# Sinkhorn block attention into a SwiGLU layer: batch 0's values over both row halves, queries drained inside Sinkhorn, one unit's x channel-major, wider weight loads

## The chip, the core and the metric

The kernel runs on one core of one Trainium2 chip. The core has TensorE (matrix products, called PE in the profile, its weight loads PEld), VectorE (DVE), ScalarE (ACT), GpSimd (POOL) and SyncE (SP, which here only issues DMAs), and 16 DMA engines that all queues share. The metric is device time in microseconds of one execution of the whole program, as the median of several runs.

## The reference

q, k and v are 4 batches x 8 heads x 768 positions x 64 channels. Each sequence is cut into 8 blocks of 96 positions. `sort_net` (8x8 for each head) goes through five Sinkhorn steps (exponential, row sum to one, column sum to one) and becomes a mixing matrix P, which mixes the blocks of k and v. Attention then runs inside each block, and the result, with the heads side by side (512 features), is the input of a gated feed-forward layer of width 1536.

```python
for _ in range(5):
    P = P - np.max(P, axis=-1, keepdims=True)
    P = np.exp(P)
    P = P / (np.sum(P, axis=-1, keepdims=True) + 1e-09)
    P = P / (np.sum(P, axis=-2, keepdims=True) + 1e-09)
k_sorted = np.einsum('bhij,bhjcd->bhicd', P, k_b)
v_sorted = np.einsum('bhij,bhjcd->bhicd', P, v_b)
scores = scale * np.matmul(q_b, k_sb.transpose(0, 1, 2, 4, 3))
attn = softmax(scores)
x = np.matmul(attn, v_sb)          # then (B*S, H*D)
out = (silu(x @ w_gate) * (x @ w_val)) @ w_out
```

Inputs and outputs are float32; the kernel works in bfloat16 with float32 sums.

## The kernel before, in words

**Layout.** Rows are (head, block) pairs: 64 of them, so a batch fills one half of the 128 partitions (`lowr`, `highr`). A mixing step is a matmul of natural rows of k or v with `rmix`, a 64x64 matrix that holds P of each head on its diagonal blocks. q is brought into the same channel-major layout by a selection matrix `sel`. For v the positions must come out on the partitions, so v is first copied to `vch` with channels outside and positions inside (`copy_v`, lines 117 to 124), and then mixed channel by channel (`v_chunk`, from line 267). k and q of batch 0 are split over both row halves already (`k0_chunk`, `q0_chunk`). Mixed v lies in `vt` with a column of ones behind each block, so that the product with the exponentials gives the softmax sums as well.

**A unit** is four blocks of two heads; a batch has eight. `scores` and `exps` (ScalarE) give the exponentials in `e_all`; `av` (line 326) multiplies with `vt`, takes a reciprocal of eight sums, and scales into `st`; x comes out with positions on the partitions and is transposed by TensorE (`x_to`, line 347) into `xt` and drained from PSUM. Later batches transpose by DMA.

**Stages.** Half a batch (384 positions) is one feed-forward stage, `ffn(0)` to `ffn(7)`: twelve gates (`gate`), twelve values (`value`) and three output products (`outp`). `merge` puts the attention of later halves between these steps at written places (numbers in units of estimated us of feed-forward work). PSUM has two double banks (`a`, `b`), three single ones (`gen`) and one (`x`).

**The head.** Until `ffn(0)` the order on TensorE, VectorE, ScalarE and GpSimd is written out by hand; later TensorE's and GpSimd's still are. GpSimd issues all loads that cast to bfloat16, in this order: v of batch 0 in two position halves (lines 108, both onto the lower 64 rows), q (first half), k in two halves, then three of its copies of v, then the gate and value weights in twelve loads of 256 columns, with the second half of q, v, k and q of batch 1, and one load of the output weights among and behind them. At most eight GpSimd loads are under way: the ninth waits for the first. ScalarE runs Sinkhorn's five exponentials with four copies of v between and behind them (lines 195 to 220); VectorE runs the sums, reciprocals and products. TensorE keeps itself busy with idle products (`dots`, `fill`), then turns P into `rmix` (`weights`, `mix_rows`), brings up q, v and k of batch 0 in chunks that VectorE and ScalarE drain, and computes four units. `early` starts the first gates and values on three of the four 128-feature slices of x while the fourth is under way; the fourth slice is the fourth unit (`av(0, 3)`).

Two lines that the rest comes back to:

```python
nc.vector.reciprocal(r_sb, o[0:C, :, :, D:D + 1])
merge(ffn(1), vs(v_chunk, 16, (3.2, 3.9, 4.7, 5.5)) + kqs(1, (6.2, 8.2, 10.3)) + ...)
```

Of the kernel before, what the change touches and what calls it, by code (L numbers as in the profile page):

```python
# [9 lines left out]
FP32 = mybir.dt.float32  # L10
# [7 lines left out]
def kernel(  # L18
# [15 lines left out]
    C = S // NB  # L34
    BH = B * H
# [38 lines left out]
    wo_sb = wpool.tile([128, NFC, DM], BF16)  # L74
# [3 lines left out]
    e_all = const.tile([C, 8, 4 * C + 32], BF16)  # L78
# [54 lines left out]
    HC = C // 2  # L133
    QC = C // 4
# [8 lines left out]

    load_v(0, 0, HC)
    load_v(0, HC, C)
# [4 lines left out]
    copy_v(nc.gpsimd, 0, lowr, 0)  # L150
    copy_v(nc.gpsimd, 0, lowr, 3)
    copy_v(nc.gpsimd, 0, lowr, 5, 8, 40, D)
    load_gv(0, 256)
    load_q0(1)
    for m in range(256, 1024, 256):
        load_gv(m, m + 256)
    load_v(1, 0, C)
    for m in range(1024, DF, 256):
        load_gv(m, m + 256)
    load_k(1, 0, C)  # L160
    load_q(1, 0, C)
    nc.gpsimd.dma_start(out=wo_sb, in_=wo_dram)

    rmix = {b: const.tile([128, 2, H, NB], BF16, name=f"rmix{b}") for b in (0, 1, "p")}
    for t in rmix.values():
        nc.vector.memset(t, 0.0)

    vts = {}

    def vt_tile(pair):  # L170
        if pair not in vts:
            t = vtp.tile([C, 2, H * NB, D + 4], BF16, name=f"vt{pair}", tag="vt")
            nc.vector.memset(t[:, :, :, D:D + 1].rearrange("p u n e -> p (u n) e"), 1.0)
            vts[pair] = t
        return vts[pair]

    for pair in range(B // 2):
        vt_tile(pair)

# [12 lines left out]

    p_ps = bank_tile("p_ps")[0:BH, 0:NB * NB].rearrange("p (i j) -> p i j", j=NB)
    for it in range(N_ITER):
        nc.scalar.activation(p_ps, p_sb if it == 0 else p_ps, AF.Exp)
        if it == 1:
            with nc.allow_low_precision("0/1 mask"):
                nc.vector.tensor_reduce(mask, id4, axis=AX.XY, op=ALU.add)
            nc.scalar.copy(sel, ident.rearrange("p (r g two) -> p two g r", g=H2, two=2))
        if it == 2:  # L200
            copy_v(nc.scalar, 0, lowr, 2, 8)
        if it == 3:
            copy_v(nc.scalar, 0, lowr, 3, 8)
        rowred = rowreds[it]
        nc.vector.reduce_sum(rowred[:, :, 0], p_ps, axis=AX.X)
        nc.vector.reciprocal(rowred, rowred)
        nc.vector.tensor_mul(p_ps, p_ps, rowred.to_broadcast([BH, NB, NB]))
        nc.vector.reduce_sum(colred[:, 0, :], p_ps.transpose([0, 2, 1]), axis=AX.X)
        nc.vector.reciprocal(colred, colred)
        if it < N_ITER - 1:  # L210
            nc.vector.tensor_mul(p_ps, p_ps, colred.to_broadcast([BH, NB, NB]))
    for lo in (0, NB // 2):
        part = slice(lo, lo + NB // 2)
        nc.vector.tensor_tensor(
            p_bf[:, part], p_ps[:, part].unsqueeze(2).to_broadcast([BH, NB // 2, H, NB]),
            colred.unsqueeze(1).to_broadcast([BH, NB // 2, H, NB]), op=ALU.mult)
    copy_v(nc.scalar, 0, lowr, 4, 8)
    copy_v(nc.scalar, 0, lowr, 5, 8, 0, 40)

# [6 lines left out]
    kqts = {}  # L226
# [22 lines left out]
    def q0_chunk(t, at, n, eng, tag):  # L249
        dst = kqt_tile(0)[:, GI * C:2 * GI * C].rearrange("p (g t r c) -> p t g r c", g=H2, t=2, c=QC)[:, t]  # L250
# [5 lines left out]
        drain(eng, dst[:, :, :, at:at + n], tp.rearrange("p l g r -> p g r l"))  # L256
# [56 lines left out]
    def exps(b, u, wide, pss):  # L313
        n = ecount[0] % 8
        ecount[0] += 2
        if wide is None:
            for two in range(2):
                nc.scalar.activation(e_all[:, n + two, 0:4 * C], pss[two][0:C, 0:4 * C], AF.Exp, scale=scale)
# [336 lines left out]
```

## Time and profile before

| | |
|---|---|
| Median of 3 runs | 248.6 us (248.59 to 248.83) |
| Profiled execution, its own time | 249.62 us |
| Span of the profiled execution (first to last instruction) | 247.7 us |
| TensorE busy | 239.4 us (97%) |
| VectorE busy | 157.1 us (63%) |
| ScalarE busy | 109.5 us (44%) |
| GpSimd busy | 51.9 us (21%) |
| Loads by GpSimd's queue | 14.16 MB written, 39.3% of 16 engines' span |
| Mean granted TensorE clock | 1.0 of full speed |

The span is shorter than the execution's own time, since something lies before the first and behind the last instruction. A busy engine is not an engine at its peak: TensorE's busy time includes the idle products of the head. In the views, L403 is line 403; `out<-in` are the tiles that an instruction writes and reads; a number in brackets is idle time of that engine just before the instruction, with what ended it. "Issue to landing" of a DMA is the time until its data is there.

### The profile page before, as it was taken

What the parts mean: (1) busy time and instruction counts of PE and PEld (TensorE: products, weight loads), DVE (VectorE), ACT (ScalarE), POOL (GpSimd) and SP (SyncE); (2) the same over time, 40 slices, a digit from 0 to 9 for tenths busy, and PEclk for the clock granted to TensorE, in tenths of its full rate; (3) what the DMA queues carried; (4) which work ended last, traced back from release to release, by engine and by line L of the source; (5) the groups of instructions that cost most, each with busy time, mean ns of one, the idle gap of its engine ahead of it and who ended that gap; (6) DMA issues with size and microseconds to landing.
All of it is one profiled execution on the core that took longest, in us unless ns stands there. A gap on an engine that the chain in (4) does not pass through costs nothing.

```text
span 247.7 us, 6185 instructions
## 1 busy us (share of the span) xinstructions
PE 239.4 (97%) x2633; PEld 140.7 (57%) x2633; DVE 157.1 (63%) x332; ACT 109.5 (44%) x186; POOL 51.9 (21%) x45
## 2 busy tenths in 40 slices
PE   8799998999999999999999999999999999999995
PEld 6375665666555556655555655565555555555543
DVE  6686789787556775857657646755764585446700
ACT  3877652453544444444642552354245334232311
POOL 5993459960049300000000000000000000000000
PEclk9999999999999999999999999999999999999999
DMA  5999999999999287010122121112111121100122
GB/s 98 214 120 181 218 191 219 194 227 215 215 164 179 41 201 173 4 42 3 45 56 52 55 62 34 44 42 78 32 42 45 39 57 54 42 21 25 42 81 88
DMA packets 39578, 24.38 MB, mean 98 GB/s; under 512 B 27712, under 2 KB 35648, under 8 KB 39104
## 3 DMA queue, kind: packets, MB, share of 16 engines
q0 software_dynamic: 21376, 14.16, 39.3%
q1 hardware_dynamic: 18176, 9.84, 13.9%
q8 instruction: 20, 0.33, 0.5%
q14 instruction: 6, 0.05, 0.1%
HBM read 28.32 MB, written 7.86 MB: 146 GB/s over the span
## 4 chain that ended last, share of the span: by engine, by line
PE 83%; DVE 9%; ACT 2%; issue 2%; DMA 2%; DVEq 0%; POOLq 0%
PE v_ps L403 23%; PE o_ps L420 23%; PE g_ps L385 22%; PE tkq L244 3%; PE av_ps L334 2%; PE qk L307 2%; DVE st L340 2%; DMA v<-in_v_dram 2%; DVE gs_sb L395 2%; DVE h L408 2%; DVE vt L222 1%; PE o_ps L436 1%; PE idle_ps L446 1%; PE tv L275 1%; ACT th_sb L393 1%
## 5 line engine op out<-in xcount | busy, mean ns | idle before, releaser
L395 DVE SCALAR_TENSOR_TENSOR gs_sb<-th_sb,g_ps 128x384 bf16<-128x384 bf16 x96 | 52.8, 550 | 51.5 <-ACT th_sb L393 48.7
L403 PE MATMUL v_ps<-xt,wv_sb 128*128 128x384 bf16 x380 | 77.3, 326 | 1.1 <-DVE st L340 0.7
L385 PE MATMUL g_ps<-xt,wg_sb 128*128 128x384 bf16 x376 | 76.7, 326 | 0.1
L393 ACT ACTIVATE th_sb<-g_ps 128x384 bf16<-128x384 f32 x96 | 47.1, 490 | 57.0 <-PE g_ps L385 54.5
L420 PE MATMUL o_ps<-wo_sb,h 128*128 128x512 bf16 x276 | 64.0, 379 | 0.0
L408 DVE SCALAR_TENSOR_TENSOR h<-v_ps,gs_sb 128x384 bf16<-128x384 f32 x96 | 53.3, 555 | 6.9
L403 PEld LDWEIGHTS <-wv_sb 128*128 128x128 bf16 x380 | 35.1, 97 | 24.9 <-issue 1.9
L385 PEld LDWEIGHTS <-wg_sb 128*128 128x128 bf16 x376 | 34.7, 97 | 23.5 <-issue 0.4
L420 PEld LDWEIGHTS <-h 128*128 128x128 bf16 x276 | 26.3, 98 | 28.9
L425 ACT COPY o_sb<-o_ps 128x512 f32<-128x512 f32 x23 | 13.5, 585 | 50.9 <-PE o_ps L420 50.9
L124 POOL COPY vch<-v 64x1536 bf16<-64x1536 bf16 (+2 forms) x11 | 28.6, 2635 | 21.1 <-DMA v<-in_v_dram 21.0
L320 ACT ACTIVATE e_all<-qk 96x768 bf16<-96x768 f32 x30 | 22.6, 802 | 7.6 <-PE qk L307 7.6
L340 DVE TENSOR_TENSOR st<-av_ps,r_sb 96x512 bf16<-96x512 f32 x32 | 21.7, 679 | 0.2
L334 PEld LDWEIGHTS <-e_all 96*128 96x128 bf16 x256 | 12.0, 97 | 4.9 <-ACT e_all L320 0.9
L334 PE MATMUL av_ps<-vt,e_all 96*128 96x65 bf16 x256 | 13.2, 193 | 0.0
L222 DVE CAST vt<-tv 96x1024 bf16<-96x1024 f32 (+1 forms) x9 | 9.8, 1096 | 2.6 <-PE tv L285 1.6
L338 DVE RECIPROCAL r_sb<-av_ps 96x8 f32<-96x8 f32 x32 | 6.4, 199 | 8.0 <-PE av_ps L334 7.9
L224 ACT CAST vt<-tv 96x1024 bf16<-96x1024 f32 (+1 forms) x9 | 8.1, 913 | 3.0 <-PE tv L285 1.8
L446 PE MATMUL idle_ps<-warm_sb 128*128 128x512 bf16 x25 | 7.7, 416 | 0.0
L222 DVE COPY oh_sb<-o_ps 128x256 f32<-128x256 f32 x1 | 0.4, 423 | 9.3 <-PE o_ps L436 9.3
L122 ACT COPY vch<-v 64x768 bf16<-64x768 bf16 (+1 forms) x4 | 5.4, 1375 | 0.7 <-DMA v<-in_v_dram 0.7
L370 POOL DMA_DIRECT2D q_scr<-in_q_dram x2 | 5.7, 3228 | 0.0
(80 smaller groups left out, 135.3 us busy)
## 6 DMA issues: line engine op xcount, KB each, us to landing
out_dram<-o_sb SPq DMA_DIRECT2D x23, 256.0 KB, 2.0
v<-in_v_dram POOLq DMA_DIRECT2D x3, 768.0 KB, 19.9
wg_sb<-in_moe_w_gate_dram POOLq DMA_DIRECT2D x6, 256.0 KB, 11.1
wv_sb<-in_moe_w_val_dram POOLq DMA_DIRECT2D x6, 256.0 KB, 11.9
wo_sb<-in_moe_w_out_dram POOLq DMA_DIRECT2D x1, 1536.0 KB, 23.8
kp<-in_k_dram POOLq DMA_DIRECT2D x2, 768.0 KB, 15.1
q_scr<-in_q_dram POOLq DMA_DIRECT2D x2, 768.0 KB, 29.9
v<-in_v_dram POOLq DMA_DIRECT2D x2, 384.0 KB, 6.4
```

The source lines that it names most:

```text
L124: eng.tensor_copy(dst, src.transpose([0, 2, 1]))
L222: nc.vector.tensor_copy(dst, src)
L320: nc.scalar.activation(e_all[:, n:n + 2, 0:4 * C], wide[0:C, :, 0:4 * C], AF.Exp, scale=scale)
L334: nc.tensor.matmul(o[:, two, i4, 0:D + 1], lhsT=e[:, i4 * C:i4 * C + 128], rhs=vt[:, 2 * g + two, half * 4 + i4, 0:D + 1], start=True, sto ...
L340: nc.vector.tensor_tensor(st.rearrange("p i two d -> p two i d"), o[0:C, :, :, 0:D], r_sb.to_broadcast([C, 2, 4, D]), op=ALU.mult)
L385: nc.tensor.matmul(g_ps, lhsT=wg_sb[:, kc, ts(m, 128)], rhs=xt[:, kc, :], start=(kc == 0), stop=(kc == NKC - 1))
L393: nc.scalar.activation(th_sb, g_ps, AF.Tanh, scale=0.5)
L395: nc.vector.scalar_tensor_tensor(gs_sb, th_sb, 1.0, g_ps, op0=ALU.add, op1=ALU.mult)
L403: nc.tensor.matmul(v_ps, lhsT=wv_sb[:, kc, ts(m, 128)], rhs=xt[:, kc, :], start=(kc == 0), stop=(kc == NKC - 1))
L408: nc.vector.scalar_tensor_tensor(h_tiles[n][:, m, :], v_ps, 0.5, gs_tiles.pop(m), op0=ALU.mult, op1=ALU.mult)
L420: nc.tensor.matmul(o_ps, lhsT=h_w[:, m, ts(t3, 128)], rhs=wo_sb[:, m, :], start=(m == 0), stop=(m == NFC - 1))
L425: nc.scalar.copy(o_sb, o_ps)
```

## The change

- **Batch 0's values.** The first 48 positions of each block go to the lower 64 rows, the other 48 to the upper, as k's did. The copy has 48 positions instead of 96 on twice the rows: ten of them in one ScalarE copy in Sinkhorn's fourth step, 38 in two GpSimd copies. Mixing takes two 64x64 products for each channel, and mixed v has its positions on partitions 0 to 47 and 64 to 111; k of batch 0 and the exponentials are laid out to match, with zeros between (112 rows instead of 96). GpSimd writes the zeros and the ones with nine memsets ahead of its copies, and one of 2048 elements behind the weights.
- **q.** Its first two chunks (48 products) stand on TensorE before the last row-sum product of Sinkhorn, and ScalarE drains both.
- **Fourth unit.** `avt` multiplies the other way round: the result has channels on the partitions and is x itself. The softmax sums come from a product with ones, spread over the channels; VectorE takes the reciprocal of all 128x384 of them and multiplies. There is no transpose and no drain. The second value of `ffn(0)` moves into `early`.
- **Loads.** Gate and value weights come in six loads of 512 columns, all ahead of v, k and q of batch 1, which are loaded in two parts each; the output weights in three.
- **Places.** In `ffn(1)` k and q of batch 1 come ahead of v; the first part of the last two batches' v moves from `ffn(3)` to the end of `ffn(2)`; some other places move.

```diff
-    load_v(0, 0, HC)
-    load_v(0, HC, C)
+    v0 = vnp.tile([128, HC, D], BF16, name="v0", tag="vn")
+    for a, rows in enumerate(halves):
+        nc.gpsimd.dma_start(out=v0[rows], in_=v_nat[0, :, a * HC:(a + 1) * HC, :])
     make_identity(nc, ident)
     load_q0(0)
     for a, rows in enumerate(halves):
         nc.gpsimd.dma_start(out=k0[rows], in_=k_nat[0, :, a * HC:(a + 1) * HC, :])
-    copy_v(nc.gpsimd, 0, lowr, 0)
-    copy_v(nc.gpsimd, 0, lowr, 3)
-    copy_v(nc.gpsimd, 0, lowr, 5, 8, 40, D)
-    load_gv(0, 256)
+    nc.gpsimd.memset(vch0[:, :, HC:], 0.0)
+    nc.gpsimd.memset(kqt0[:, 0:NK].rearrange("p (n c) -> p n c", c=64)[:, :, HC:], 0.0)
...
+    copy_v0(nc.gpsimd, 10, 29)
+    copy_v0(nc.gpsimd, 29, HC)
+    load_gv(0, 512)
     load_q0(1)
-    for m in range(256, 1024, 256):
-        load_gv(m, m + 256)
-    load_v(1, 0, C)
-    for m in range(1024, DF, 256):
-        load_gv(m, m + 256)
-    load_k(1, 0, C)
-    load_q(1, 0, C)
-    nc.gpsimd.dma_start(out=wo_sb, in_=wo_dram)
+    load_gv(512, 1024)
+    load_gv(1024, DF)
+    nc.gpsimd.memset(vch[lowr, D * 64:D * C], 0.0)
+    load_v(1, 0, HC)
+    load_v(1, HC, C)
+    for lo, hi in ((0, 64), (64, C)):
+        load_k(1, lo, hi)
+        load_q(1, lo, hi)
+    for n in range(3):
+        nc.gpsimd.dma_start(out=wo_sb[n], in_=wo_dram[:, n * 4:(n + 1) * 4, :])
...
+    def v0_chunk(at, n, eng, tag):
+        tp = chunk_tile("tv0", n // 8, tag).rearrange("p (l n) -> p l n", n=H * NB)
+        for ld in range(n):
+            for a, rows in enumerate(halves):
+                nc.tensor.matmul(tp[rows, ld, :], lhsT=vch0[rows, at + ld, :],
+                                 rhs=rmix[0][rows, a].rearrange("p h i -> p (h i)"),
+                                 start=True, stop=True)
+        drain(eng, vts[0][0:KC, 0, :, at:at + n], tp[0:KC].transpose([0, 2, 1]))
...
+    def avt(u, tag):
+        half, g = divmod(u, H2)
+        vt = vts[0][0:KC, 0].rearrange("p (h i) e -> p h i e", h=H)
+        ps = pair_tile("avt_ps", tag)
+        for two in range(2):
+            nc.tensor.matmul(ps[two * D:(two + 1) * D, 512:512 + TW], lhsT=ones_sb[0:KC],
+                             rhs=es[(0, u)][two][:, 0:TW], start=True, stop=True)
+        for i4 in range(4):
+            for two in range(2):
+                nc.tensor.matmul(ps[two * D:(two + 1) * D, i4 * C:(i4 + 1) * C],
+                                 lhsT=vt[:, 2 * g + two, half * 4 + i4, 0:D],
+                                 rhs=es[(0, u)][two][:, i4 * C:(i4 + 1) * C], start=True, stop=True)
+        total = opool.tile([128, DM], FP32, name="total", tag="o_sb")[:, 0:TW]
+        x = xts[(0, half)][:, g, :]
+        nc.vector.reciprocal(total, ps[:, 512:512 + TW])
+        nc.vector.tensor_tensor(x, ps[:, 0:TW], total, op=ALU.mult)
...
+        if it == 3:
+            copy_v0(nc.scalar, 0, 10)
...
+        if it == N_ITER - 1:
+            early_q = [q0_chunk(0, 0, 16, "s", "b"), q0_chunk(0, 16, 8, "s", "a")]
+            for f in early_q:
+                f()
...
-    q0_chunk(0, 0, 16, "s", "b")
-    v_chunk(0, 0, 8, "v", "gen")
-    v_chunk(0, 8, 8, "s", "gen")
-    v_chunk(0, 16, 16, "v", "a")
-    v_chunk(0, 32, 8, "v", "gen")
-    v_chunk(0, 40, 16, "s", "b")
-    v_chunk(0, 56, 8, "s", "gen")
+    v0_chunk(0, 8, "v", "gen")
+    v0_chunk(8, 8, "s", "gen")
+    v0_chunk(16, 16, "v", "a")
+    v0_chunk(32, 16, "s", "b")
+    v0_chunk(48, 8, "s", "gen")
+    v0_chunk(56, 8, "v", "gen")
     k0_chunk(0, 16, "v", "a")
     k0_chunk(16, 16, "s", "b")
-    k0_chunk(32, 8, "v", "gen")
-    k0_chunk(40, 8, "s", "gen")
-    q0_chunk(0, 16, 8, "v", "a")
+    k0_chunk(32, 4, "v", "gen")
+    k0_chunk(36, 4, "s", "gen")
+    k0_chunk(40, 8, "s", "a")
...
-    av(0, 3, "b")
+    avt(3, "a")
...
-    x3 = xt_tile("x", 1)
-    x_to(x3[:, 0], 0, 3)
-    drain("v", xts[(0, 0)][:, 3:4, :], x3.rearrange("p g a b -> p g (a b)"))
     early(0, (2,))
     early(1, (2,))
-    early(2, (0,))
-    early(0, (3,))
-    early(1, (3,))
-    early(2, (1, 2, 3))
+    early(2, (0, 1))
+    for n in range(2):
+        early(n, (3,))
+    early(2, (2, 3))
+    early(3, (0, 1, 2, 3))
...
-    merge(ffn(1), vs(v_chunk, 16, (3.2, 3.9, 4.7, 5.5)) + kqs(1, (6.2, 8.2, 10.3))
-          + units(1, range(4), (11.3, 16.4), (3.1, 2.5)))
+    merge(ffn(1), kqs(1, (5.9, 7.2, 11.1)) + vs(v_chunk, 16, (8.5, 9.1, 9.8, 10.4))
+          + units(1, range(4), (12.3, 17.0), (3.1, 2.4)))
...
-    merge(ffn(2), units(1, range(4, 8), (0.0, 5.5)) + kqs("p", (13.0, 16.2, 19.4))
+    merge(ffn(2), units(1, range(4, 8), (0.0, 5.5)) + kqs("p", (13.0, 14.7, 20.7)) + v_pairs([(0, 22.5)])
           + [(13.0, lambda: q_dma(2)), (16.4, lambda: q_dma(3))])
-    merge(ffn(3), v_pairs([2.6 * n for n in range(4)]) + units(2, range(4), (9.8, 14.0)))
+    merge(ffn(3), v_pairs([(1, 0.0), (2, 5.1), (3, 6.9)]) + units(2, range(4), (9.8, 14.0)))
```

## The prediction

> **What bounds the kernel now.** I read the page first, then the chain of waits over the first 30 us, the timeline of ScalarE, GpSimd and TensorE there, the landings of the first loads, and the gaps between TensorE instructions after that. The first lines are the page's (span, busy time of each engine) and the chain's (start, duration, what):
>
> ```profile
> span 247.7 us, 6185 instructions
> PE 239.4 (97%) x2633; PEld 140.7 (57%) x2633; DVE 157.1 (63%) x332; ACT 109.5 (44%) x186; POOL 51.9 (21%) x45
> ...
> 6.54 1.51 ACT vch L122
> ...
> 11.51 0.29 PE w_ps L463 x4
> ...
> 13.27 0.69 DVE vt L222
> ...
> 23.00 0.34 PE x_ps L351 x4
> ```
>
> TensorE is the bound: 239.4 of 247.7 us, at a granted clock of 1.00 in every stretch asked for. From 25.4 us on (gates and values back to back) I summed the gaps between matmul starts that exceed the column time by over 0.1 us: 4.2 us. That is all that moved loads and retimed steps can recover. The rest of the change lies in the head before 25.4 us, where the chain runs through v's load, ScalarE's copies, Sinkhorn, the v, k and q drains, four units and the fourth unit's x. Next, timeline rows (start, duration, what; idle time before it and its cause), with the landings of v's first two loads among them:
>
> ```profile
> 6.57 6.34 POOL L124 COPY vch<-v 64x1536 bf16<-64x1536 bf16 x3 [1.97 <-DMA v<-in_v_dram]
> ...
> 7.94 0.20 ACT L195 ACTIVATE p_ps<-p_ps 32x64 f32<-32x64 f32 x1
> ...
> 9.63 0.19 ACT L195 ACTIVATE p_ps<-p_ps 32x64 f32<-32x64 f32 x1
> 9.75 2.43 ACT L122 COPY vch<-v 64x768 bf16<-64x768 bf16 x2
> ...
> DMA to landing us min/median/max: 5.2/6.4/7.5
> ...
> 10.46 1.04 PE L446 MATMUL idle_ps<-warm_sb 128*128 128x512 bf16 x4
> ...
> 12.83 0.84 PE L275 MATMUL tv<-rmix,vch 64*128 64x64 bf16 x23
> ...
> 41.99 0.28 PEld L403 LDWEIGHTS <-wv_sb 128*128 128x128 bf16 x3 [0.84 <-DMA wv_sb<-in_moe_w_val_dram]
> ```
>
> See three things. v's two loads (issued at 1.28 and 1.92) land after 5.2 and 7.5 us, at 6.5 and 9.4: today the copies start on the first half. The v matmuls start at 12.83, as the Sinkhorn weights are ready. And a weight load stands 0.84 us for the last value columns, issued at 26.9 and landed 15.1 us later.
>
> **The change part by part.** The sum is a difference, made in the profiled execution (span 247.7, its own time 249.62, so 1.9 us lie around it) and put onto the median of 248.6, 1.0 below that execution.
>
> *v over both halves.* GpSimd's copy fits 0.20 us + 1.70 ns an element (2.81 at 1536, 0.69 at 288, the same at 64 and 128 rows), so two of 1216 cost 4.5 us in place of 6.34; ScalarE's (1.49 at 768, 1.00 at 480) makes 1.27 at 640, in place of 5.4 in four. But every copy now spans both halves, so it waits for 9.42, not 6.5. GpSimd ends at 13.95 (12.91 before). ScalarE's copy stands in front of the fifth exp: 9.42 + 1.27 puts that exp at 10.7 instead of 9.63, and all behind it (p_bf at 12.9, not 11.78). GpSimd's nine new memsets (2,600 elements; 0.25 us at 128 against 0.10 at one gives 1.2 ns each, the copy's 1.7 is the other end) take 3.4 to 4.9 us from 4.6: hidden by the wait, 0.1 late at worst. The two ones-memsets leave VectorE, where they stood before Sinkhorn's first exp: nothing.
>
> *q drained inside Sinkhorn.* TensorE now has 48 q matmuls ahead of the last row-sum matmul and its fill. q lands 7.8 us after its issue at 3.00, so 10.8; 48 matmuls took 0.95, and from the row-sum matmul (10.34) to the first weights matmul (11.51) are 1.17: weights start at 13.0, end at 13.65, the two mask products (0.47) end at 14.15. The v matmuls start at 14.2: **+1.35 us**. Three bounds (q on TensorE, the exp on ScalarE, GpSimd's 13.95) lie within 0.3, so none helps alone. The two q drains (1.01 on ScalarE and 0.69 on VectorE before, among v's and k's) run on an idle ScalarE.
>
> *From v to the first scores.* Before, 12.83 to 18.59: 5.76. VectorE drains 4.3 us in place of 5.0, ScalarE 4.0 in place of 4.7. But order and buffers pass it on. v doubles to 128 matmuls; those with alternating row halves took 18 ns each (L285), those on one half 29. From the start S: second VectorE drain (1024 columns) S+1.35 to 2.57; k's first 32 matmuls want its bank, to S+3.27; k's second 32, whose drain is ScalarE's, to S+3.92; then 1.01, 0.35 and 0.58 to S+5.94, scores at S+6.1 = 20.3 (18.59 before): **+1.7**. Ends: 5.0 if the drains pack, 7.5 if 128 matmuls cost 31 ns each.
>
> *Fourth unit.* The four units' exps are a ScalarE chain that does not change: its last ends at 24.2 (22.50). Before, av, reciprocal 0.20, product 0.69, transposes 0.34 and drain 0.36 gave x at 24.74. Now two 384-column sums (0.16 to 0.33 us), 8 matmuls of 96 columns, a reciprocal of 128x384 and a product (0.555, the row of that shape). The reciprocal decides, and its price at 384 columns is not in the trace:
>
> ```profile
> L338 DVE RECIPROCAL r_sb<-av_ps 96x8 f32<-96x8 f32 x7 | 1.4, 200 | 1.5 <-PE av_ps L334 1.5
> ...
> L205 DVE TENSOR_REDUCE rowred<-p_ps 32x8 f32<-32x64 f32 x5 | 1.1, 212 | 1.4 <-ACT p_ps L195 1.4
> ...
> L209 DVE RECIPROCAL colred<-colred 32x8 f32<-32x8 f32 x5 | 1.0, 191 | 0.2
> ```
>
> Other VectorE work out of PSUM costs 0.149 us + 1.04 ns a column (1024 in 1.216, 64 in 0.22). By that 8 columns take 0.157; the reciprocal takes 0.199. If all above 0.149 is a price per column, it is 6.2 ns and 384 take 2.55 us (colred's 0.191 over the 0.129 that an SBUF source leaves fixed gives 7.75 ns, 3.1 us). If the excess is fixed, 384 take 0.6. I take 2.55, by the row of the same operation on the same memory. x is ready at 24.65 + 2.55 + 0.6 = 27.8, against 24.74; TensorE has done eight matmuls instead of seven (0.16): **+2.9** where the stream starts. At 0.6, x comes at 25.85 and TensorE itself is behind at 26.3: +1.35.
>
> [...] No row here has a long reciprocal.
>
> *Weights in 512 columns, ahead of batch 1.* Issues go from twelve of some 0.77 us to six, starting at 13.95 (12.85). The first pair, twice as large, lands at 13.95 + 5.5 (the first pair's time, 12.85 to 13.63 + 4.7) + 2.6 (0.52 MB more at the 199 GB/s of 24 to 28 us) = 22.1; used from 24.9. The last pair lands at 34 to 35 in place of 42.0, so the 0.84 us wait goes. VectorE is next there (no idle from 38.3 to 42.9): I take **-0.75**, ends -0.3 and -0.86. Behind the weights, GpSimd's 2048-element memset (2.4 to 3.7 us) stands ahead of v1, k1, q1 and the output weights, which wait for earlier landings anyway; each of these waits holds what follows on that queue. v1 lands near 38, its four copies (11.17) end near 49, not 46.2; k1 and q1 by 46, the output weights by 54 (56.2). Against their first uses (k1 near 51, v1 near 56 by its later place, output weights at 58) all is hidden; without that cover it is one for one. kp, v2 and the q scratch casts go 3 us later into the queue behind loads that finish earlier. On SP no issue changes its order.
>
> [...] Here the stretch of 256 KB weight loads (24 to 28 us) ran at 199 GB/s and that of the 1.5 MB output weights (46 to 52 us) at 211.
>
> *Retimed steps.* k1 before v1, later units, batch-2 v begun in the previous stage. The other gaps after 25.4 total 3.3 us; those near moved steps (at 53.7, 55.7, 62.4, 65.3 and 69.4: 1.47; from 113 to 127: 1.06) 2.5. Which vanish the trace can't say: **-0.9**, ends -2.5 and, as new waits are possible, +0.5.
>
> Sum: +2.9 - 0.75 - 0.9 = +1.25: **249.8 us**.
>
> **Rivals.**
> - *The reciprocal costs a column time per element.* For it: the excess over 0.157 is only 0.042 us, and a fixed part can't be told from eight columns. Then +1.35 - 1.65 = -0.3: 248.3, not slower. It decides from about 1.3 us downward, where the sum crosses zero; below 0.9 it gives nothing more.
> - *The retimed steps stall anew.* VectorE is packed until 42.9; three k chunks and v drains pushed together could hold PSUM. +2.9 - 0.75 + 0.5, with a reciprocal near 3: 251.3.
> - *The first weights come late.* For it: the median weight landing is 11.9 us after issue, which from 14.7 is 26.6, 1.7 us after use. Against: the first pair took 4.1 and 4.7. Behind a slow reciprocal it hides (26.6 and eight matmuls of 0.16 end at 27.9, as x comes); behind a cheap one it puts the same 27.9 in its place: 249.9.
>
> **How the numbers follow.** Forecast 0.50 (own range 248.8 to 251.0), cheap reciprocal 0.33 (247.0 to 249.3; 0.16 of it faster, 0.10 same), new stalls 0.12 and late weights 0.05 (both slower). Under 247.4 is the lower tail of the cheap reciprocal, over 251.7 that of the new stalls with a reciprocal over 3 us: range 247.4 to 251.7. Changes within 0.2% (0.5 us, about what a measurement here can tell) count as the same. With 0.03 faster and 0.04 same from the forecast's own lower end: faster 0.19, same 0.14, slower 0.67.
>
> **What would show it.** The fifth exp near 10.7, the v matmuls near 14.2, scores near 20.3; one reciprocal of 128x384 over 2 us with TensorE idle for over 1 us at 26; no weight load waiting for a value-weight DMA. I am wrong if v's second load lands well before 9.4, if that reciprocal is under 1 us, or if the gaps after 30 us sum to under 1.5 us.

## The result, and the profile after

The changed kernel takes 254.38 us (median of 3 runs) against 248.59 for the kernel before (4 runs on the same chip): 2.3% slower, ratio 1.0231, 95% interval 1.0211 to 1.0251. A fourth run took 258.28 us in a slower state of the core, at a mean granted clock of 0.987; such runs are left out of the medians, ratios and intervals here and below. The forecast was 249.8 with a range to 251.7. The profiled execution's own time is 254.4, so here profile and median agree.

The page of the changed kernel, its first lines, and then pieces of its chain of waits in the head (start, duration, what):

```profile
span 252.6 us, 6285 instructions
PE 237.0 (94%) x2669; PEld 140.3 (56%) x2695; DVE 158.2 (63%) x328; ACT 106.9 (42%) x185; POOL 54.3 (22%) x53
```

```profile
9.59 4.47 POOL vch L158 x2
14.10 1.22 PE tv L282 x64
...
16.97 0.72 issue
...
23.09 1.14 issue
...
26.63 2.57 DVE total L369
```

TensorE's share falls from 97% to 94% while its work hardly changes. Two pieces are called "issue": TensorE waits there for no semaphore, no DMA and no other engine that the profile shows. The same stretch in the timeline (start, duration, what; idle time before it and its cause), ScalarE and GpSimd first, then TensorE:

```profile
9.59 4.46 POOL L158 COPY vch<-v 128x1216 bf16<-128x1216 bf16 x2 [0.53 <-DMA v<-in_v_dram]
...
9.50 1.28 ACT L156 COPY vch<-v 128x640 bf16<-128x640 bf16 x1 [1.84 <-DMA v<-in_v_dram]
10.68 0.20 ACT L484 ACTIVATE p_ps<-p_ps 32x64 f32<-32x64 f32 x1
...
14.10 2.21 PE L282 MATMUL tv<-rmix,vch 64*64 64x64 bf16 x128 [0.66 <-POOL vch L158]
16.62 0.35 PE L261 MATMUL tk<-rmix,qk 128*64 128x64 bf16 x11 [0.30 <-DVE vt L219]
17.70 1.27 PE L261 MATMUL tk<-rmix,qk 128*64 128x64 bf16 x69 [0.72 <-issue]
...
22.82 0.27 PE L345 MATMUL av_ps<-vt,e_all 112*128 112x65 bf16 x3
24.22 0.33 PE L345 MATMUL av_ps<-vt,e_all 112*128 112x65 bf16 x5 [1.14 <-issue]
...
29.83 0.32 PE L573 MATMUL g_ps<-xt,wg_sb 128*128 128x384 bf16 x1 [1.57 <-DVE xt L370]
...
42.00 0.34 PE L317 MATMUL qk<-kqt 64*128 64x96 bf16 x8 [0.63 <-DVE st L351]
```

The fifth exp starts at 10.68, the v products at 14.10, both as forecast. TensorE then stops within a chunk of k, after 11 of its products, and within the second `av`, after 3 of its 8: in the middle of runs of equal instructions, where nothing is waited for. Before the last slice of x it stands 1.57 us for VectorE, which does this (one row of the groups: busy, mean ns):

```profile
L369 DVE RECIPROCAL total<-avt_ps 128x384 f32<-128x384 f32 x1 | 2.6, 2558 | 0.3 <-PE avt_ps L364 0.3
```

2.56 us, where 2.55 was forecast. No weight load waits for value weights any more (their last load lands at 35.46), but at 42.00, where it used to wait for one, a score product waits 0.63 us for VectorE. That is a new wait.

Where the time went, by points that both kernels pass. The base is a second profile of the kernel before (run e10 below: own time 248.47, span 246.5), since the first lay 1 us over the median. The tanh times are starts of the gates' tanh on ScalarE, twelve to a stage:

```
point                          before   after    later by   added in this stretch
first product of the weights    11.20   12.87     1.67       1.67
first scores                    18.30   20.87     2.57       0.90
first tanh                      24.84   30.19     5.35       2.78
13th tanh (stage 0 done)        44.09   50.47     6.38       1.03
49th tanh (stages 1 to 3)      136.07  141.91     5.84      -0.54
end of the span                246.52  252.63     6.11       0.27
```

The last 0.27 lie behind the last output's landing, not in the work.

### The profile page after: what moved, and what is told of

Read it like the earlier page. It is cut to its first block, busy times and chain, and to the rows that moved or that the text cites. A ratio compares the mean times of both kernels' runs of the same rounds, so it can differ in the third digit from the quotient of the medians.

```text
span 252.6 us, 6285 instructions
## 1 busy us (share of the span) xinstructions
PE 237.0 (94%) x2669; PEld 140.3 (56%) x2695; DVE 158.2 (63%) x328; ACT 106.9 (42%) x185; POOL 54.3 (22%) x53
## 4 chain that ended last, share of the span: by engine, by line
PE 81%; DVE 7%; issue 4%; DMA 3%; POOL 2%; ACT 2%; POOLq 0%; DVEq 0%; ACTq 0%
PE v_ps L431 23%; PE g_ps L413 23%; PE o_ps L448 22%; DMA v<-in_v_dram 3%; PE tkq L241 3%; PE av_ps L345 3%; PE qk L317 2%; POOL vch L158 2%; DVE gs_sb L423 1%; DVE st L351 1%; DVE h L436 1%; PE o_ps L464 1%; DVE total L369 1%; ACT th_sb L421 1%; PE idle_ps L474 1%
## 5 line engine op out<-in xcount | busy, mean ns | idle before, releaser
L431 PE MATMUL v_ps<-xt,wv_sb 128*128 128x384 bf16 x376 | 76.5, 326 | 0.6 <-DVE gs_sb L423 0.5
L421 ACT ACTIVATE th_sb<-g_ps 128x384 bf16<-128x384 f32 x96 | 47.1, 491 | 60.8 <-PE g_ps L413 56.8
L448 PE MATMUL o_ps<-wo,h 128*128 128x512 bf16 x254 | 61.9, 379 | 1.3 <-issue 0.3
L331 ACT ACTIVATE e_all<-qk 96x768 bf16<-96x768 f32 (+1 forms) x30 | 22.6, 803 | 8.5 <-PE qk L317 8.5
L127 POOL COPY vch<-v 64x1536 bf16<-64x1536 bf16 (+1 forms) x8 | 22.4, 2853 | 11.8 <-DMA v<-in_v_dram 11.8
L345 PEld LDWEIGHTS <-e_all 96*128 96x128 bf16 (+1 forms) x248 | 11.6, 98 | 6.1 <-issue 1.3
L345 PE MATMUL av_ps<-vt,e_all 96*128 96x65 bf16 (+1 forms) x248 | 12.8, 193 | 1.2 <-issue 1.1
L219 DVE CAST vt<-tv 96x1024 bf16<-96x1024 f32 (+2 forms) x9 | 9.8, 1098 | 2.4 <-PE tv L293 1.7
L221 ACT CAST vt<-tv 96x1024 bf16<-96x1024 f32 (+2 forms) x9 | 8.1, 916 | 7.0 <-PE tv L293 3.6
L474 PE MATMUL idle_ps<-warm_sb 128*128 128x512 bf16 x21 | 6.3, 405 | 0.7 <-issue 0.7
L317 PEld LDWEIGHTS <-kqt 64*128 64x128 bf16 x128 | 3.0, 94 | 4.0 <-issue 1.8
```

The lines of the kernel that those rows point to most:

```text
L127: eng.tensor_copy(dst, src.transpose([0, 2, 1]))
L219: nc.vector.tensor_copy(dst, src)
L331: nc.scalar.activation(e_all[K, n:n + 2, 0:4 * C], wide[K, :, 0:4 * C], AF.Exp, scale=scale)
L345: nc.tensor.matmul(o[:, two, i4, 0:D + 1], lhsT=e[:, i4 * C:i4 * C + 128], rhs=vt[:, 2 * g + two, half * 4 + i4, 0:D + 1], start=True, sto ...
L421: nc.scalar.activation(th_sb, g_ps, AF.Tanh, scale=0.5)
L431: nc.tensor.matmul(v_ps, lhsT=wv_sb[:, kc, ts(m, 128)], rhs=xt[:, kc, :], start=(kc == 0), stop=(kc == NKC - 1))
```

## The experiments

The theory after this result had three parts: the two unexplained stalls are late instructions, the reciprocal costs what TensorE waits for x, and something in the middle eats what the loads and places bring. All ratios below are against runs of the kernel before on the same chip; a ratio is worked out from the single runs and need not be that of the two medians.

**e1, e2: the fourth unit.** e1 takes the unit back:

```diff
-    avt(3, "a")
+    av(0, 3, "a")
...
+    x3 = xt_tile("x", 1)
+    x_to(x3[:, 0], 0, 3)
+    drain("v", xts[(0, 0)][:, 3:4, :], x3.rearrange("p g a b -> p g (a b)"))
```

> The changed kernel with the fourth unit alone put back: av on the 112 rows, reciprocal of 112x8, product, four transposes, drain by VectorE. Theory: what the change of this unit costs on the path is the time TensorE stood for x, 1.57 us in the changed kernel's timeline; old way from last exp to x took 2.24 us before, so x comes at 25.95 + 2.24 = 28.2 in place of 29.78, and the time goes from 254.4 to 252.8 (252.4 to 253.3). Rival: something later (VectorE, batch 1's loads) limits anyway, so the 1.6 us are given back: within 0.4 us of 254.4. In both cases the two stalls of TensorE without a releaser, in the k matmuls and in the second av, stay where they are at 17.0 and 23.1 us (0.7 to 0.9 and 1.1 to 1.3 us), as nothing ahead of them is touched.

e2 leaves only the reciprocal out, with a plain copy in its place, so that x of this unit is not divided by the sums:

```diff
-        nc.vector.reciprocal(total, ps[:, 512:512 + TW])
+        nc.vector.tensor_copy(total, ps[:, 512:512 + TW])
```

> The changed kernel with the 128x384 reciprocal replaced by a plain copy of the same tile (the fourth unit's x is then multiplied by its total in place of being divided, so the output differs there). Theory: the copy takes 0.149 + 384 x 1.04 ns = 0.55 us in place of 2.56; x comes at 27.8; TensorE has work of its own until about 28.2, so its 1.57 us of idle go and the time is 252.8 (252.4 to 253.2). Rival, the reciprocal is covered by something else that is late: under 0.4 us gained, 254.0 to 254.4.

Measured: e1 252.13 us (ratio 1.0118, 1.0072 to 1.0165), e2 252.17 (1.0119, 1.0071 to 1.0166): 2.3 and 2.2 us off, not nothing, so the reciprocal is on the path. In e2's TensorE timeline the early products run on without a gap:

```profile
27.09 0.33 PE L573 MATMUL g_ps<-xt,wg_sb 128*128 128x384 bf16 x1
27.25 0.33 PE L573 MATMUL v_ps<-xt,wv_sb 128*128 128x384 bf16 x1
27.41 0.65 PE L573 MATMUL g_ps<-xt,wg_sb 128*128 128x384 bf16 x3
```

Most of the surplus over 1.6 need not be the unit's: in both profiles the q products start 0.3 to 0.4 us earlier than in the changed kernel's (10.48 and 10.57 against 10.90), as q's load lands at another moment (10.44 and 10.53 against 10.86). Both stalls stood where they were, at 16.5 to 17.3 and 22.3 to 23.9 us, again after 11 k products and 3 of the second `av`.

**e3, e4: what are the stalls without a cause?** The stalls stand before products 351 and 479 of TensorE's program, counted in the code from the first warm-up product (a float32 one counts as two: the four on `rowred` have eight weight loads and eight matmuls in the trace): 128 products apart, and each is two instructions, a weight load and a matmul. So the number of warm-up products at the start, which run while TensorE has nothing to do, is changed from 124 to 156 (e3) and 92 (e4).

```diff
-    dots(124)
+    dots(156)
```

> The changed kernel with 156 in place of 124 of the small warm-up matmuls at the start (32 more, 64 TensorE instructions, run while TensorE waits anyway). Instruction theory: TensorE's program comes in blocks of 256 instructions, 128 matmuls with their weight loads; the two stalls without a releaser stand before matmul 351 and matmul 479 of the program, exactly 128 apart, so they are late blocks. Then both stalls must come 32 matmuls earlier in the program: before v matmul 108 of 128 (at about 16.0 us) and in the first scores (before about the 8th to 12th matmul of them, at about 20.5 us), none in the k matmuls after their 11th and none inside the second av. The block before matmul 319 is then asked for in the q matmuls at 11.8, 2.4 us earlier than its like now, so the first stall shrinks to 0 to 0.4; the second has 4 us in place of 6 to be fetched, 0.5 to 2 us: time 252.5 to 254.8. Rival, the stalls belong to a place in the work (a PSUM bank, the SBUF port, e_all): they stay after the 11th k matmul and inside the second av, 0.7 to 0.9 and 1.1 to 1.3 us, and the time stays at 254.4 within 0.4.

> The changed kernel with 92 in place of 124 warm-up matmuls. Instruction theory: both stalls come 32 matmuls later in the program: before the 44th k matmul (0.5 to 0.9 us, at about 17.6 us) and, in place of the second av, between the third av and the fourth unit's matmuls at about 25 us, where the block has had 2 us more to come, so 0 to 0.5 us: time 253.2 to 254.2. Rival, place in the work: stalls stay after the 11th k matmul and inside the second av, time 254.4 within 0.4.

TensorE in e3, then in e4:

```profile
16.50 1.46 PE L261 MATMUL tk<-rmix,qk 128*64 128x64 bf16 x80 [0.31 <-DVE vt L219]
...
19.85 0.34 PE L317 MATMUL qk<-kqt 64*128 64x96 bf16 x7
21.68 0.55 PE L317 MATMUL qk<-kqt 64*128 64x96 bf16 x17 [1.49 <-issue]
...
23.49 0.42 PE L345 MATMUL av_ps<-vt,e_all 112*128 112x65 bf16 x8
```

```profile
16.43 0.86 PE L261 MATMUL tk<-rmix,qk 128*64 128x64 bf16 x43 [0.31 <-DVE vt L219]
18.61 1.01 PE L261 MATMUL tk<-rmix,qk 128*64 128x64 bf16 x53 [1.33 <-issue]
...
22.94 0.42 PE L345 MATMUL av_ps<-vt,e_all 112*128 112x65 bf16 x8
```

32 more products ahead and the second stall comes 32 products earlier, after 7 score products instead of 3 of the second `av`; the first is gone (0 to 0.4 was expected at the 108th v product). 32 fewer and the first comes 32 later, after 43 k products instead of 11; the second is gone. The place in the work is refuted, the count of instructions is what fixes them. As times, e4 gains more than expected, 252.53 us (1.0139, 1.0096 to 1.0183), and e3 loses, 255.93 (1.0265, 1.0213 to 1.0316) where 252.5 to 254.8 was expected; e3's profiled execution took 254.55, the others 255.8 to 256.7 at a mean clock of 0.992 to 0.993, of which more below. A new stall of 0.55 us also stood in e3's batch-1 v products, at 62 us, 4 x 128 products after the one at 21.68.

The trace's DMA records fit a block of 256 instructions. One of the two queues marked "instruction" moves 21 packets of 16 KB in the changed kernel, and TensorE has 5,377 instructions in the records, 21.0 times 256. A packet follows each block start in the stretch in question. The page's line of that queue (packets, MB, share of 16 engines' span):

```profile
q8 instruction: 21, 0.34, 0.5%
```

Read as the fetch of the block that comes after the one just started, a packet gives (times in us; the block start is counted in the code, the packet is from the DMA records):

```
                        block starts   packet starts   takes   first instruction of the next block
after, first stall         14.30          15.08        1.16     17.70
after, second stall        17.70          21.82        0.89     24.22
e3 (156)                   15.85          19.35        0.97     21.68
e4 (92)                    14.45          16.41        0.97     18.61
```

From the packet's end to the first instruction 1.2 to 1.5 us. From block start to packet 0.8 us when the DMA engines are idle (a share of 0.00 from 14 to 15 us in the changed kernel), 2.0 when the weights have just started, 3.5 to 4.1 when they run (1.24 from 17.7 to 21.8; 4.5 us in e1, from 16.96 to 21.43).

**e7: the same in the kernel before.** If instructions are the cause, the old kernel is as vulnerable.

```diff
-    dots(124)
+    dots(60)
```

> The kernel before with 60 in place of 124 warm-up matmuls, nothing else. Instruction theory: blocks of 128 matmuls with their weight loads; counted from the starts seen in the changed kernel, the block starts of this one are at matmuls 351 and 479 of the old numbering shifted by 64: before the 28th k matmul (about 15.8 us) and before the 44th after it on (first av of unit 0, about 19.9 us). The first is asked for at v matmul 27 to 91 and may be 0 to 1 us late, the second has only 4 us in a stretch where the DMA engines are full, so TensorE stands without a releaser for 1 to 2.5 us at the first av: 249.6 to 251.2. Rival, that the unexplained stalls belong to the changed kernel's own work (112 rows, row halves): none here, 248.6 within 0.3.

252.26 us (1.0136, 1.0056 to 1.0215). Its TensorE timeline, then stretches of it (stretch, length, busy of PE, PEld, DVE, ACT, POOL; granted clock, DMA share, GB/s):

```profile
20.65 0.27 PE L334 MATMUL av_ps<-vt,e_all 96*128 96x65 bf16 x3
22.58 0.33 PE L334 MATMUL av_ps<-vt,e_all 96*128 96x65 bf16 x5 [1.66 <-issue]
```

```profile
22.60:24.20 1.60, 1.60 (x31) 1.13 (x32) 1.19 (x4) 0.77 (x2) 0.77 (x2) 1.00 1.45 196
24.20:27.40 3.20, 3.20 (x26) 2.00 (x23) 1.76 (x4) 1.38 (x3) 2.00 (x3) 0.51 1.45 198
```

The stall is there, 1.66 us, in the second `av` (the expectation had miscounted to the first; product 415 is the fourth of the second). The time is above the 249.6 to 251.2 that was expected: another stall of 1.13 us stands at 60.75, 4 x 128 products later, and a stretch at half clock follows the first. So the kernel before had this danger too and its number of warm-up products happens to hide it. The second view shows why the price is above the stall: 1.7 us after it TensorE's granted clock is 0.50 for 3.4 us. By an estimate that alone is up to 1.7 us, and one such stretch in 251 us is a mean clock of 0.993, the value that several runs here show.

**e8, e9: is it the weights' traffic that makes a block late?** e8 makes GpSimd wait for the third unit's exp before the second and third pair of weights, e9 for the first k drain before all of them.

```diff
-    load_gv(512, 1024)
...
     qk(0, 2, "gen")
+    nc.gpsimd.tensor_copy(held_sb, es[(0, 2)][1][0:32, 0:8])
+    load_gv(512, 1024)
```

```diff
-    load_gv(0, 512)
...
     k0_chunk(16, 16, "s", "b")
+    nc.gpsimd.tensor_copy(held_sb, kqt0[0:32, 0:8])
+    load_gv(0, 512)
```

> The changed kernel with GpSimd made to wait for the third unit's exp (about 23.5 us) before it issues the second and third weight loads and all that follows; the first pair is issued as it was. Theory: an instruction block waits in the DMA engines behind the weights. The block for the second av is asked for at 17.7; the first pair alone is through at about 20, so its packet starts by 20 in place of 21.8 and the second stall (1.14 us) is under 0.4 or gone, while the first, asked for on idle DMA engines at 14.3, stays at 0.5 to 0.9. Rival, the time to fetch a block is fixed and has nothing to do with the loads: second stall 1.0 to 1.4 us as it was. What the late loads cost after 30 us is not the question; the time may go up.

> The changed kernel with GpSimd made to wait for the first k drain (about 19.4 us) before it issues the first weight load, and all later loads behind it in the old order. Theory: a block of TensorE instructions asked for while the DMA engines are full waits 3.5 to 4.5 us for its packet, on idle ones 0.8 to 1.1; then 0.95 us for the packet and 1.2 to 1.4 until the first instruction. The block for the second av, asked for at about 17.5, now meets idle engines: its packet starts by 18.6, it is there by 21, and TensorE needs it at about 22.8, so the second stall is gone; the first, asked for at 14.2, shrinks to 0.3 to 0.7. The first pair of weights lands at 25.5 and 28, behind the slow x at about 28.4, so it costs nothing there; x about 1.3 us earlier than in the changed kernel, 253.1 if the 5 us later batch-1 loads stay covered, up to 2 us more if they do not. Rival, a block always takes some 6.5 us from one to the next: second stall 1.0 to 1.4 us as it was.

e8 (255.73; 1.0263, 1.0174 to 1.0353) misses: the first stall grew to 1.89 us, as GpSimd was done half a microsecond sooner, the first weight load was issued at 13.51 instead of 14.00 and the block's packet came behind it, at 16.48. The second stall is gone, but by then TensorE was later anyway, and the first pair alone landed as late as 22.26. It does not tell the theories apart. e9 does. Its TensorE:

```profile
18.89 1.27 PE L249 MATMUL tk<-rmix,qk 128*64 128x64 bf16 x69 [0.78 <-issue]
...
24.02 0.42 PE L333 MATMUL av_ps<-vt,e_all 112*128 112x65 bf16 x8
...
30.07 0.50 PE L575 MATMUL v_ps<-xt,wv_sb 128*128 128x384 bf16 x2 [2.76 <-DMA wv_sb<-in_moe_w_val_dram]
```

The block that starts at 18.89 meets idle DMA engines: its packet starts at 19.95, 1.06 us later instead of 4.1, and the second `av` runs through. The fixed time per block is refuted. The first stall stays, 0.78 us: its block, too, meets idle engines (the DMA share from 14.4 to 18 us is 0.02), so here 128 products in 2.4 us outran even a block that had no load to wait behind. The time of e9, 256.09 us (1.0304, 1.0248 to 1.0361), is above the expected 253 to 255: the first value weights now come 2.76 us late, and TensorE's wait for q, 1.51 us, was followed by 3.4 us at half clock (0.50 from 11.0 to 14.4).

**e5, e6, e10: the middle, and the base.** e6 gives the kernel before only the new loads of weights and batch 1, e5 also the new places (the diff under e12, the other way round), the early value step (the second value of stage 0 among the early products; under e13, the other way round) and the output weights in three loads.

```diff
-    for m in range(256, 1024, 256):
-        load_gv(m, m + 256)
-    load_v(1, 0, C)
...
+    load_gv(512, 1024)
+    load_gv(1024, DF)
+    load_v(1, 0, HC)
```

> The kernel before with only what the change does after the head: weights in 512 columns ahead of batch 1, batch 1 in halves, output weights in three loads, the value of the second column block among the early matmuls, retimed k1, v1 and batch-2 v steps. Head (v, q, fourth unit) as before. Forecast's theory: the terms -0.75 and -0.9 hold and were only hidden in the changed kernel: 247.0 (246.0 to 247.6). Rival, read from the changed kernel's trace: the load wait of 0.84 us goes, but VectorE is as late in its place (0.80 us at a score matmul for st, 0.33 and 0.46 for gs), so the sum is nothing: 248.6 within 0.4.

> The kernel before with the loads alone: weights in 512 columns ahead of batch 1, batch 1 in halves, all steps at their old places. Forecast's theory: the last value columns land near 34, the 0.84 us wait goes, 247.9 (247.6 to 248.4), and the batch-1 v copies and k1/q1 come about 3 us later but in time. Rival: v1 comes later than its old places ask (v matmuls of batch 1 from about 47 us, copies now ending near 49), and TensorE waits there for GpSimd, 1 to 3 us: 249 to 251.

> The kernel before once more, to see what the forecast's base was. Its profiled execution lay 1.0 us over the median of the runs. If the 0.84 us wait of a weight load for the last value columns belongs to that execution alone, a profile with a time of 248.6 shows a span of 246.7 and no such wait at 42 us, and the -0.75 of the forecast was taken from a stall that the usual run does not have. If the wait is in every run, this profile shows it again (0.7 to 0.9 us), and the 1.0 us lies elsewhere in the head.

e6: 249.48 (1.0009, 0.9979 to 1.0040), no gain. Its median lies in the rival's 249 to 251, but the rival's wait is not in its profiled execution (248.65 us): from the 13th to the 49th tanh that takes 92.07 us, against 91.98 in e10. e10 says why there is no gain. The kernel before in an execution of 248.47 us, its span and its weight loads near 42 us:

```profile
span 246.5 us, 6185 instructions
...
41.98 0.64 PEld L403 LDWEIGHTS <-wv_sb 128*128 128x128 bf16 x4
```

There is no wait: the last value weights land at 38.32, against 41.95 in the execution that was profiled first, and stage 0 takes 19.25 us instead of 20.12. So the 0.84 us load wait of the forecast is not in an execution near the median, which the forecast was put on. e6's profiled execution has the same span, 246.6. The eight runs of e10, all of one kernel, range from 248.40 to 251.85, median 250.02 (1.0049, 1.0013 to 1.0085 against its own like): a difference of half a per cent is not clear of the noise here, whatever its interval. What the longer runs wait for was not profiled; they may have the load wait again. e5 (252.07; 1.0112, 1.0063 to 1.0161) fell outside both expectations: its profile has a stall of 2.0 us with no releaser at 56.8, half clock behind it, and stage 0 takes 20.28 us instead of 19.25.

**e11, e12: both found costs out.** The fourth unit as before and 92 warm-up products; e12 also with the old places.

```diff
-    merge(ffn(1), kqs(1, (5.9, 7.2, 11.1)) + vs(v_chunk, 16, (8.5, 9.1, 9.8, 10.4))
-          + units(1, range(4), (12.3, 17.0), (3.1, 2.4)))
+    merge(ffn(1), vs(v_chunk, 16, (3.2, 3.9, 4.7, 5.5)) + kqs(1, (6.2, 8.2, 10.3))
+          + units(1, range(4), (11.3, 16.4), (3.1, 2.5)))
```

> The changed kernel with the fourth unit as before and 92 warm-up matmuls: both found costs out together. If they add: 254.4 - 1.9 - 2.2 = 250.3 (249.9 to 250.9), what is left over 248.6 being the later v, k and scores (some 2 us) less what the middle recovers. If the instruction block only moves to another dense place, TensorE shows a stall without a releaser of over 1 us elsewhere and the time is 251 to 252.

> The same as the kernel with both costs out, with the batch-1 and batch-2 steps back at the places they had before (v of batch 1 ahead of k, batch-2 v only in the fourth stage, output steps after columns 6, 9, 11). Forecast's theory: the new places are worth 0.9 us, so this one is 0.9 slower, 251.2. Rival, from the runs on the kernel before (loads alone, and loads with new places, apart by 0.5 us once the instruction stall is taken off): the new places cost 0.3 to 0.7 us, so this one is 249.6 to 250.0, its gaps of TensorE after 30 us 0.3 to 0.7 us less.

252.54 us (1.0122, 1.0052 to 1.0191) and 252.20 (1.0133, 1.0084 to 1.0182): the gains did not add, and the two are not told apart by their times. The stall after 43 k products was 2.31 us in e11's profile and 0.78 in e12's, though the head is the same program: the first weight load was issued at 13.52 in e11 and the block's packet started at 17.38, in e12 at 13.96 and 15.42. The runs of e11 lie at 251.0 and 251.2 or, at a clock of 0.993, at 253.9. The stages are steadier: from the 13th to the 49th tanh e11 takes 91.45 and e12 92.08, so the new places save 0.63 us (less in e1 and e13, where these stages take 91.73 and 91.82). The rival there, which had the places cost time, is wrong; the loss in e5, its stall and the half clock apart, must lie in stage 0.

**e13, e14, e15: the value step, and the places without it.** e13 is the changed kernel with that step back in the stream; e14 the kernel before with new loads and places but without the step; e15 the same with `dots(140)`.

```diff
-    early(3, (0, 1, 2, 3))
...
-    value_out(0, 1, first[3])
...
-            if n > 0 or m > 1:
+            if n > 0 or m > 0:
                 todo.append((0.65, lambda m=m: value(n, m)))
```

> The changed kernel with one step put back: the value of the second column block of batch 0 (four matmuls and its product on VectorE) in the stream after the early matmuls, where it was before. Theory, read from the stages of all traces: the stage from the first to the thirteenth tanh takes 20.28 us in every kernel that has that step among the early matmuls and 19.25 in those that have not (a load wait of 0.86 apart), by a stall of 0.80 us at a score matmul that waits for the product st and 0.33 at one for gs; the stage falls to 19.2 to 19.4, the two stalls go, and the time is 253.4 (253.2 to 253.8). Rival: the stalls come from the later loads or the fourth unit's new order and stay, stage 20.1 to 20.4, 254.4 within 0.3.

> The kernel before with the loads in 512 columns and the new places of k1, v1, the units and batch-2 v, but without the early value step. Theory: first stage 19.25 us as in the kernel before; the next three stages together 0.5 to 0.6 us shorter than the 92.0 of the kernel before, if no block of instructions is late there; but the new places put the k and v matmuls of batch 1 close together while the output weights and the next loads fill the DMA engines, and the kernel before with all of the middle stood 2.0 us for a block at 56.8 us: if it does so again, 249.5 to 252 with the halved clock behind it; if not, 248.0. Rival: the new places cost time by themselves, stages 0.3 to 0.7 us longer without any stall without a releaser.

> The same with 140 warm-up matmuls: every block starts 16 matmuls earlier in the program. Instruction theory: a stall in the k matmuls of batch 1 comes 16 matmuls earlier (in the first chunk, after some 36 to 48 matmuls of it) and is 0 to 1.3 us in place of 2.0, as 16 dense matmuls fewer lie in the block before it; in the head the block starts move to the 76th k matmul and the transposes of the first units, 0 to 1 us. Time 248.0 to 250.5. Rival: the stall at 56.8 us belongs to the place, the end of a k chunk ahead of a gate, and stays there with 1.8 to 2.2 us.

e13: 252.70 us (1.0151, 1.0105 to 1.0198), 1.7 less than the changed kernel, of which some 0.5 is a shorter second stall in its profile (0.59). Its stage 0 takes 18.59 us, below the 19.2 to 19.4 that were expected, and 0.4 us of that is lost again in stages 1 to 3. The score products that waited at 42.00 run through:

```profile
38.72 0.58 PE L317 MATMUL qk<-kqt 64*128 64x96 bf16 x16
```

The clean price is e5 against e14, which differ in this step alone: stage 0 takes 20.28 and 19.25, 1.03 us. The same score products in e5, then in e14:

```profile
36.77 0.34 PE L308 MATMUL qk<-kqt 64*128 64x96 bf16 x8 [0.64 <-DVE st L341]
```

```profile
34.72 0.57 PE L308 MATMUL qk<-kqt 64*128 64x96 bf16 x16
```

Why VectorE is late there is read from the code: `merge` counts the main steps that it has put out; with the value gone from its list every unit comes one step later in the stream, while VectorE owes the product of that value on top, and a score product finds its bank still held.

e14: 251.05 (1.0076, 1.0034 to 1.0117); e15: 248.19 (0.9985, 0.9965 to 1.0004). TensorE in the batch-1 k products of e14, then of e15:

```profile
52.59 1.20 PE L245 MATMUL tkq<-rmix,kq 128*64 128x64 bf16 x64
55.75 0.83 PE L386 MATMUL g_ps<-xt,wg_sb 128*128 128x384 bf16 x4 [1.96 <-issue]
```

```profile
52.44 1.20 PE L245 MATMUL tkq<-rmix,kq 128*64 128x64 bf16 x64
53.58 0.82 PE L386 MATMUL g_ps<-xt,wg_sb 128*128 128x384 bf16 x4
...
59.10 0.63 PE L245 MATMUL tkq<-rmix,kq 128*64 128x64 bf16 x28
59.95 0.76 PE L245 MATMUL tkq<-rmix,kq 128*64 128x64 bf16 x36 [0.21 <-issue]
```

Sixteen warm-up products more, and the stall of 1.96 us behind the second k chunk is gone. A block of e15 starts after some 48 products of that chunk, and nothing waits there; 128 products later, after 28 of the third chunk, a stall of 0.21 us is left. The expectation had named the first chunk. e15 is the lowest median of all, 0.3 us under the 248.52 of the kernel before beside it; the interval still holds 1, so it is not shown to be faster.

## Why the prediction was wrong

Three terms of the sum failed. It charged nothing for bringing TensorE's instructions, which cost some 2.2 us; it charged nothing for the value step moved among the early products, which costs 1.03 us; and it took 0.75 us off for a load wait that an execution near the median does not have. The reciprocal, on which the rivals turned, was right.

- *v over both halves, q inside Sinkhorn* (+1.35): right. Fifth exp 10.68 for 10.7, v products 14.10 for 14.2, behind GpSimd's copies as one of the three bounds. Against e10's execution of the kernel before it is +1.57.
- *From v to the first scores* (20.3): the mechanism was right and would have given 20.0. It came out at 20.87 through the first stall, which took 0.89 us off the products' pace. The step that failed is its cost of the 128 products: their duration was right (17 ns each, 18 forecast), but nothing was charged for bringing 256 instructions to TensorE in 2.2 us.
- *Fourth unit* (+2.9 with the rest of the head): the reciprocal was 2.56 for 2.55. That it has a price for each column was the right reading, and the rival of a cheap one is dead; that 42 ns over eight columns gave 384 columns to 0.01 us is in part luck. It is on the path, and costs what TensorE waits, 1.57 us. "The last exp ends at 24.2" failed: 25.95, by the first stall's 0.9 and by 1.1 to 1.3 us of the second.
- *Weights in 512 columns* (-0.75): the landings were right or nearly so (22.29 for 22.1, 35.46 for 34 to 35, output weights 54.03 for 54). Against an execution near the median the gain was zero: the wait stood in the one execution that was read, and the sum was put on a median without it. e6 and e10 show it.
- *Retimed steps* (-0.9): the places are worth 0.54 to 0.63. The failing step is one that the sum left out: the value of stage 0 moved among the early products was costed at nothing, and it costs 1.03 us (e5 against e14).
- The rivals had no late instructions and no price for the value step; the second had new waits for VectorE, but at the k and v steps of later stages and at +0.5. Late instructions alone, some 2.2 us by an estimate from the two stalls, would have put the time outside the range.

The miss, in spans against e10: 6.11 measured, 1.25 forecast. Stalls some 2.2, the load wait 0.75, the value step 1.03, places 0.36, and what remains, 0.5, in small terms of the head and behind the end.

The 128 products between stalls, each of two instructions, and the 21 packets for 5,377 instructions agree with blocks of 256 instructions. TensorE stood for them 0.72, 1.14, 1.33, 1.49, 1.66, 1.96 and 2.31 us in the runs above; in the table that is where the 128 products before a stall were through in less than the time from one block's start to the next one's first instruction, 3.4 to 6.5 us.

## What to carry to other kernels

A stall of TensorE called "issue", in the middle of equal instructions and with nothing to wait for, may be instructions that are late: count products from the program's start, look for distances of 128, and shift them with a few harmless products to test it. Many small matmuls in a row outran the blocks here even on idle DMA engines (0.78 us in e9), and more so where large loads filled them (1.14 us in the changed kernel at the second `av`, which runs through in e9). An edit that adds or removes instructions early moves the later block starts (32 products moved the stalls by 32 in e3 and e4), so two versions that differ by sixteen harmless products (e14 251.05 us, e15 248.19) can differ by some 1% for that reason. Profile the base twice before a wait in it is booked as gain, and cost every step that a hand-written schedule counts, also the one that only leaves a list.

## What had not been expected of the hardware

- The instruction blocks: in the table, e1 and e9, 0.8 to 1.1 us from a block's start to its packet on idle DMA engines and 3.5 to 4.5 us beside the weight loads, then some 1 us for the packet and 1.2 to 1.5 us to the first instruction that had waited for it. That the packet belongs to the next block is inferred from its time and from the counts; no record names it.
- A TensorE gap of 1.4 to 2.3 us was followed, within 0.4 to 1.7 us, by one stretch of 3.41 us at a granted clock of 0.50 in e1, e5, e7, e8, e11 and e14, and a gap of 1.51 us was in e9; but none came after 1.49 us in e3's profiled execution, 1.57 us in the changed kernel's, 1.76 us in e8's wait for q or 2.76 us in e9's for value weights. What decides between the two was not settled.
- The float32 reciprocal on VectorE, out of PSUM, took 2.56 us for 384 columns, 6.3 ns a column over the 0.149 us that other work there shows as fixed, against 0.56 us for the product of the same shape. The row of the eight-column reciprocal, 0.20 us, had led to the right figure, 2.55.
